# Two-bank score passes on VectorE, a re-tuned plan and a residual added on VectorE in an adaLN transformer block

## The chip, the cores and the metric

The kernel runs on one core of one Trainium2 chip. The metric is the device time of one execution in microseconds (us); less is better. Three runs of the kernel before gave 745.32, 745.73 and 746.55 us, median 745.73.

In the profile the engines are called PE (TensorE, the matmuls), PEld (its weight loads), DVE (VectorE), ACT (ScalarE), POOL (GpSimd) and SP (the engine that issues most DMAs). "L1279" is line 1279 of the kernel before.

## What is computed

A transformer block with adaptive layer norm: 2048 tokens of width 512, 32 heads of width 16, a hidden width of 1376. All inputs are bf16.

```
mod = (silu(c) @ w_mod).reshape(1, 6, 1, 512)         # sa, ca, ga, sb, cb, gb
h = layernorm(x) * (1 + ca) + sa
q, k, v = heads(h @ wqkv)
p = softmax(q k^T * 16 ** -0.5)
x = x + ga * ((p v) @ wo)
h = layernorm(x) * (1 + cb) + sb
x = x + gb * (gelu(h @ w1 + b1) @ w2 + b2)
```

## The kernel before, in words

**Streams and tiles.** The attention is cut into 32 streams, numbered `qi` 0 to 31. One stream is one block of 512 queries (four blocks `b`), one chunk of eight heads (four chunks `ch`), and the even or the odd heads of it; the four heads of a stream lie in four row groups of TensorE. The last four streams (`halved`) are cut otherwise: 256 queries, even and odd heads together. A stream has 16 key tiles of 128 keys. One tile (stream, key tile) gives four PSUM banks of scores, 128 keys x 512 queries each, one for each head. In all there are 32 x 16 = 512 tiles. The softmax is taken without its maximum: the exponential of the scores is multiplied with the values, which carry a column of ones for the sum, and the sum divides later.

**Two ways to the exponential.** Most tiles are done by ScalarE: PE writes two score banks (`issue_unit`, L991; matmuls at L923), and one ScalarE instruction takes the exponential of both (L1279, `act`). The banks of ScalarE are the pairs 0, 1 and 3, 4. The other tiles, chosen from the six key tiles in `DKT`, are done by VectorE: PE writes one score bank at a time into one of the "flex" banks 2, 5, 6 and 7 (`d_next` and `d_issue`, L946 to L982), and VectorE turns it into 16-bit integers, whose bits read as float16 are roughly the exponential (`p_pass`, L1338, instruction at L1350). When the four rows of a tile are done, three shifted copies of it are made by adding an integer (`emit_shift`, L1301; on VectorE at L1321, on GpSimd at L1327), and all four versions are multiplied with values scaled to match (`VE` and `VV`), so that the error of the rough exponential averages out. A tile on VectorE so takes four value matmuls for each row where one on ScalarE takes one. The flex banks also hold the output accumulators of the streams (`open_o`) and the banks of all other matmuls (`x_open`).

**Who decides the order.** The order of the instructions is written by a planner while the kernel is built: a small simulation (loop at L1530) with a clock for PE, ScalarE, VectorE and GpSimd and fixed costs for each operation (L54 to L78). At each step the engine that is free first picks its next work by a fixed policy: `pe` (L1154), `act`, `dve` (L1486), `pool`. VectorE takes copies of finished outputs first, then evacuations of other matmuls, then reciprocals, score passes, tasks and last shifts. GpSimd takes a shift only where VectorE has at least `POOL_MIN` us of other work in sight. What the chip then runs is this fixed order on each engine, with semaphores between them; which tile is done by ScalarE and which by VectorE is fixed by it too.

Around the attention the planner places the projections, layer norms, the up and down projections of the three earlier query blocks ("jobs" with matmuls, "tasks" without). Each has a gate, a position in the row of tiles from which it may start (`K_GATE`, `Q_GATE`, `X1_GATE`, `U_GATE`, `OUT_GATE`, `U2_GATE`, `OUT2_GATE`, `Z_GATE`). The thresholds of the policy are constants that a table may overrule for single turns; a turn (`next_turn`, L828) is half a stream of tiles, so the table `TURNS` (L38) has keys from 0 to 63:

- `D_AHEAD`: how early, before VectorE is out of work, PE may give a turn to scores for VectorE alone (L1172)
- `D_WAIT`: how much time PE must have until ScalarE needs its next banks for it to do so (L1173)
- `D_STOP`: how many tiles of a stream must be left for VectorE to begin one (L960)
- `OPEN_N`: how many value matmuls must be ready for the next stream's accumulator to be opened (L1029)
- `X_LEAD`: shifts the position against which gates are compared (L839)

**Pairs.** `p_pass` already has the code for passes over two banks: where the next waiting bank is ready, is the next higher one (`i + 1`), and holds the next row of the same tile, one instruction does both. `PAIR = False` (L85) turns it off. In the planner a pass costs 0.602 us and a pair 1.135 us.

**Fills.** Where PE has nothing to do for a while, `fill` (L1098) issues four matmuls with zero weights into an open accumulator. It needs all four rows of that stream to have started.

**The tail.** `last_tail` (L1581) does what is left after the last exponential, written out by hand, with a generator of filler matmuls (the up and down projections of the first 256 of the last 512 tokens), of which `gap(GAPS[i])` issues so many at each place. For the last two token tiles of 128 (`tt` 2 and 3) the output projection starts before the end of the attention, in the jobs "z" (L792): `outer` adds the residual `x` by a matmul with the identity and then the first three head chunks, in one bank for each token tile (`pz`). In the tail the last chunk is added (L1637, `W_z`), so that the bank holds the whole new `x`. VectorE takes the layer norm statistics straight from the bank (L1640), GpSimd the root (L291, L292), and the two tiles are normalised from the banks by ScalarE (L1648) and VectorE (L1649) side by side. After transposes and copies (L1655 to L1658) VectorE casts the two banks into `xr` (L1661), which the last adds read (L1683).

Of the kernel before, what the change touches and what calls it, by code (L numbers as in the profile page):

```python
# [21 lines left out]
P = 128  # L22
# [14 lines left out]

TURNS = {29: {'D_AHEAD': 0.3}, 30: {'D_AHEAD': 0.3}, 31: {'D_AHEAD': 0.3}, 32: {'D_AHEAD': 0.3}, 47: {'OPEN_N': 10}, 48: {'OPEN_N': 10}, 60: {'D_STOP': 5}, 61: {'D_STOP': 5}, 62: {'D_STOP': 5}, 63: {'D_STOP': 5}}  # L38
TURN = 2
# [7 lines left out]
D_FROM = 0  # L47
D_AHEAD = 0.1
D_STOP = 4
# [34 lines left out]
Q_POOL = False  # L84
PAIR = False  # L85
K_GATE = (-1.7, 0.25)
Q_GATE = -1.1
X1_GATE = (0.3, 1.3)
U_GATE = (1.7, 5.0)
OUT_GATE = (5.0, 7.9)  # L90
OPEN_N = 14
# [8 lines left out]
NARROW = False  # L100
GAPS = (10, 4, 0, 12, 2, 3, 9, 3)
NHQ = 4
# [4 lines left out]
XA_AT = 30.5  # L107
U2_GATE = (1.7, 5.0)
OUT2_GATE = (4.6, 7.2)
LOAD_AT = (2, 3)  # L110
D_END = 6
BULK_LEFT = 8
Z_GATE = 0.2

# [49 lines left out]
def adaln_block(ctx: ExitStack, tc: tile.TileContext, A_x, A_wqkv, A_wo, B_x, B_w1, B_b1, B_w2, B_b2,  # L164
# [81 lines left out]
    def bank(i):  # L246
        return PS[:, i, :]
# [82 lines left out]
    def copy(eng, dst, src):  # L330
        if eng == AC:
            nc.scalar.copy(out=dst, in_=src)
        else:
            nc.vector.tensor_copy(out=dst, in_=src)
# [332 lines left out]
    def plain(ps, lhsT, rhs, start, stop):  # L667
        nc.tensor.matmul(out=ps, lhsT=lhsT, rhs=rhs, start=start, stop=stop)  # L668
# [123 lines left out]
    for tt in range(2, 4):  # L792
        job(("z", tt), NQ - Z_GATE + 0.001 * tt, ["xl1"] + [ot_key(ch, 1) for ch in range(3)],
            [lambda ps, tt=tt, i=i: outer(bank(ps), tt)[i]() for i in range(4)], [], mode="full")
    xa, ha = hT[:, 0:2, 0:512], hT[:, :, 512:768]
# [25 lines left out]
    dcount = [0] * NQ  # L821
    st = {"ap": 0, "cur": None, "mode": None, "unit": 0, "lastpe": 0.0, "expd": 0}

# [17 lines left out]
    def halved(qi):  # L841

        return qi >= NQ - NHQ
# [310 lines left out]
    def pe(now):  # L1154
# [426 lines left out]
    def last_tail():  # L1581
# [57 lines left out]
        for t in range(2):  # L1639
            nc.vector.bn_stats(out=st2[:, 2 + t, :], in_=bank(pz[t]))  # L1640
# [8 lines left out]
        nc.vector.tensor_scalar(out=hns[0], in0=bank(pz[0]), scalar1=mv[:, 0, 0:1], scalar2=rs[:, 0:1],  # L1649
                                op0=ALU.subtract, op1=ALU.mult)  # L1650
        both = [PS[:, k, :].bitcast(BF16).rearrange("p (j n) -> p j n", n=256) for k in (kd, kr)]
# [193 lines left out]
```

## Time and profile before

| what | us |
|---|---|
| median of three runs | 745.73 |
| the profiled execution, its own time | 744.98 |
| span of its profile, first to last instruction | 743.1 |
| start of the first exponential of the attention | 13.0 |
| start of the last exponential | 716.31 |
| VectorE's score passes (L1350), first and last start | 52.8, 707.0 |

The span is what the engines show; the profiled execution's own time is 1.9 us more. A row of the page's groups reads: line, engine, operation, output and inputs with their shapes, how many; then busy time in all and the mean of one in ns; then the idle time of the engine just before these instructions and what ended most of it. A row of the timeline begins with its start and its length in us. A row of a stretch gives its length, and for each engine the busy time and the number of instructions in it, then the granted clock of TensorE as a share of full speed, the share of DMA and GB/s.

### The profile page before, as it was taken

To read this page: it belongs to the slowest core of one execution; us is meant where nothing else is said; L and a number is where in the kernel's file an instruction comes from. 1 tells how busy PE (TensorE), PEld (TensorE's weight loads), DVE (VectorE), ACT (ScalarE), POOL (GpSimd) and SP (SyncE) were. 2 spreads that over 40 slices of the span, in tenths; PEclk is the share of its full clock that TensorE was granted. 3 is DMA by queue.
4 is the path that set the end of the run, shared out by engine and by line. 5 is a ranking of instruction groups with operands and counts; after the bars stand their busy time and mean duration, and the time that the engine had idled before them with its cause. 6 is when DMAs were issued, how large, how long until landed. Compare 5 with 4: busy or idle time off the path is not lost.

```text
span 743.1 us, 22039 instructions
## 1 busy us (share of the span) xinstructions
PE 726.6 (98%) x9017; PEld 236.6 (32%) x9020; DVE 681.2 (92%) x1188; ACT 718.4 (97%) x776; POOL 421.5 (57%) x263
## 2 busy tenths in 40 slices
PE   8999999999999999999999999999999999999998
PEld 3323323232333222222222222322232222434455
DVE  8958899999999999999999999999999999989973
ACT  4999999999999999999999999999999999999993
POOL 3102756766565566676777465765667668653620
PEclk9999999999999999999999999999999999999999
DMA  8600001011120100001200200000010200000111
GB/s 279 168 10 2 25 4 24 22 56 48 45 65 11 38 10 22 7 16 24 53 17 10 44 4 15 12 18 24 18 50 5 46 10 9 19 27 22 41 27 32
DMA packets 42859, 25.57 MB, mean 34 GB/s; under 512 B 27609, under 2 KB 37906, under 8 KB 42754
## 3 DMA queue, kind: packets, MB, share of 16 engines
q1 hardware_dynamic: 41938, 23.01, 11.8%
q8 instruction: 72, 1.18, 0.6%
q10 hardware_dynamic: 816, 1.12, 0.4%
q14 instruction: 33, 0.27, 0.1%
HBM read 16.58 MB, written 2.61 MB: 26 GB/s over the span
## 4 chain that ended last, share of the span: by engine, by line
ACT 51%; PE 36%; issue 9%; DVE 3%; POOL 1%; DMA 0%; ACTq 0%; POOLq 0%; DVEq 0%
ACT pB L1279 25%; ACT pA L1279 25%; PE PS L1087 12%; PE PS L923 12%; PE PS L254 8%; PE PS L668 3%; DVE t L1350 1%; DVE t L1321 1%; POOL t L1327 1%; ACT uG L728 1%; DVE qm L341 1%; PE PS L1104 1%; DMA cc_bf<-in_c_dram 0%; DVE st L281 0%; PE PS L300 0%
## 5 line engine op out<-in xcount | busy, mean ns | idle before, releaser
L1327 POOL TENSOR_SCALAR t<-t 128x2048 int16<-128x2048 int16 x192 | 363.2, 1897 | 244.1 <-DVE t L1321 112.1
L1279 ACT ACTIVATE pA<-PS 128x1024 bf16<-128x1024 f32 x368 | 397.6, 1080 | 2.3 <-PE PS L923 1.8
L1279 ACT ACTIVATE pB<-PS 128x1024 bf16<-128x1024 f32 x368 | 398.2, 1082 | 0.4 <-PE PS L923 0.3
L1350 DVE TENSOR_SCALAR t<-PS 128x512 int16<-128x512 f32 x576 | 370.7, 680 | 26.9 <-PE PS L923 23.9
L923 PE MATMUL PS<-qm,kT 32*128 32x512 bf16 x2048 | 305.1, 383 | 7.3 <-ACT pA L1279 2.6
L1087 PE MATMUL PS<-t,VV 128*32 128x512 f16 (+1 forms) x1956 | 225.0, 359 | 1.7 <-POOL t L1327 1.6
L923 PEld LDWEIGHTS <-kT 32*128 32x128 bf16 x2048 | 86.8, 91 | 286.4 <-issue 282.3
L1321 DVE TENSOR_SCALAR t<-t 128x2048 int16<-128x2048 int16 x240 | 175.1, 755 | 0.5 <-PE PS L1087 0.2
L1087 PE MATMUL PS<-pA,VE 128*32 128x512 bf16 (+1 forms) x826 | 168.3, 361 | 0.0
L1087 PE MATMUL PS<-pB,VE 128*32 128x512 bf16 (+1 forms) x826 | 164.3, 361 | 0.0
L1087 PE MATMUL PS<-t,VE 128*32 128x512 f16 (+1 forms) x652 | 133.8, 359 | 1.4 <-DVE o_sb L1386 1.0
L1087 PEld LDWEIGHTS <-VE 128*32 128x32 bf16 x2304 | 70.1, 94 | 77.5 <-issue 72.6
L1087 PEld LDWEIGHTS <-VV 128*32 128x32 bf16 x1956 | 64.7, 95 | 58.3 <-issue 52.0
L254 PE MATMUL PS<-h2T,W 128*32 128x512 bf16 x528 | 42.7, 383 | 0.0
L254 PE MATMUL PS<-W,uG 128*32 128x512 bf16 x528 | 41.6, 394 | 0.0
L1104 PE MATMUL PS<-kT,zeros 128*32 128x512 bf16 x296 | 28.4, 383 | 0.0
L1465 POOL TENSOR_TENSOR OT<-o_sb,rb 128x512 bf16<-128x512 f32 (+1 forms) x17 | 20.0, 1177 | 14.5 <-DVE t L1321 11.8
L719 DVE TENSOR_SCALAR uG<-PS,b1c 128x512 bf16<-128x512 f32 x33 | 24.5, 742 | 1.7 <-PE PS L254 1.4
L341 DVE TENSOR_SCALAR qm<-PS,qmask 128x512 bf16<-128x512 f32 x32 | 22.6, 741 | 2.2 <-PE PS L254 2.2
L291 POOL TENSOR_SCALAR rs<-mv 128x4 f32<-128x4 f32 (+1 forms) x10 | 3.7, 371 | 34.6 <-DVE mv L286 34.1
L254 PE MATMUL PS<-hT,W_k 128*32 128x512 bf16 x256 | 21.2, 383 | 0.5 <-DVE hT L324 0.5
L254 PE MATMUL PS<-hT,W_q 128*32 128x512 bf16 x256 | 20.9, 383 | 0.0
(132 smaller groups left out, 362.9 us busy)
## 6 DMA issues: line engine op xcount, KB each, us to landing
rb<-d SPq DMA_DIRECT2D x112, 32.0 KB
W_m<-in_w_mod_dram SPq DMA_DIRECT2D x2, 1024.0 KB
out_dram<-ob SPq DMA_DIRECT2D x15, 128.0 KB
o_sb<-o SPq DMA_DIRECT2D x56, 32.0 KB
xb<-in_A_x_dram SPq DMA_DIRECT2D x3, 512.0 KB
xr<-in_A_x_dram SPq DMA_DIRECT2D x3, 512.0 KB
W<-in_B_w_dram SPq DMA_DIRECT2D x4, 344.0 KB
W<-in_B_w_dram SPq DMA_DIRECT2D x5, 256.0 KB
```

Source lines behind the costliest of these rows:

```text
L254: nc.tensor.matmul(out=ps[32 * g:32 * g + 32, :], lhsT=lhsT[:, 32 * g:32 * g + 32], rhs=rhs, start=start, stop=stop)
L341: nc.vector.tensor_scalar(out=qm[(b, ch)][:, par, :], in0=ps, scalar1=qmask[:, par:par + 1], scalar2=None, op0=ALU.mult)
L668: nc.tensor.matmul(out=ps, lhsT=lhsT, rhs=rhs, start=start, stop=stop)
L719: nc.vector.tensor_scalar(out=X["u"][:, fc, :], in0=bank(ps), scalar1=late["b1c"][:, fc:fc + 1], scalar2=None, op0=ALU.add)
L923: nc.tensor.matmul(out=dst, lhsT=kT[rows, ch, kt * P:(kt + 1) * P], rhs=rhs, start=True, stop=True)
L1087: nc.tensor.matmul(out=bank(O[qi])[32 * r:32 * r + 32, cs], lhsT=w, rhs=rhs[:, cs], start=(n == 1 and not halved(qi)), stop=last and (pr = ...
L1104: nc.tensor.matmul(out=bank(O[qi])[32 * r:32 * r + 32, :], lhsT=zeros[:, 0:32], rhs=kT[:, 0, 0:512], start=False, stop=False)
L1279: nc.scalar.activation(out=t[:, 0:n, :], in_=PS[:, b0:b0 + n, :], func=ACT.Exp, scale=math.log(2.0) / STEP)
L1321: nc.vector.tensor_scalar(out=t16[:, rs, :], in0=d["tile"][:, rs, :], scalar1=float(MJ[j]), scalar2=None, op0=ALU.add)
L1327: nc.gpsimd.tensor_scalar(out=t16[:, rs, :], in0=d["tile"][:, rs, :], scalar1=1.0, scalar2=float(MJ[j]), op0=ALU.mult, op1=ALU.add)
L1350: nc.vector.tensor_scalar(out=d["tile"][:, r:r + n, :], in0=PS[:, i:i + n, :], scalar1=T_BIAS, scalar2=0.0, op0=ALU.add, op1=ALU.max)
L1465: nc.gpsimd.tensor_tensor(out=ot[:, 0:w], in0=o[:, 0:w], in1=rb[:, 0:w], op=ALU.mult)
```

## The change

- `PAIR = True`: one VectorE pass over two neighbouring banks where both are ready.
- Constants anew: `D_AHEAD` 0.2 for 0.1, a little in the gates, `GAPS` with one filler matmul moved from the late place to the place ahead of the transposes, and another table `TURNS`: entries for turns 17 to 20, 37 to 40, 45, 46 and 55 to 59 in place of 29 to 32, 47, 48 and 60 to 63.
- The residual of the last two token tiles: the identity matmul in `outer` goes; in the tail VectorE adds bank and `xr` into `xr`, takes the statistics from there, and normalises both tiles from there; the product for ScalarE's bias, ScalarE's normalisation and the two casts go.
- `extra_fill`: where PE has been idle for over 0.3 us and nothing else was possible, four zero matmuls into the accumulator of one of the last four streams, also where not all its rows have started. The planner's clock doesn't count them.

```diff
-TURNS = {29: {'D_AHEAD': 0.3}, 30: {'D_AHEAD': 0.3}, 31: {'D_AHEAD': 0.3}, 32: {'D_AHEAD': 0.3}, 47: {'OPEN_N': 10}, 48: {'OPEN_N': 10}, 60: {'D_STOP': 5}, 61: {'D_STOP': 5}, 62: {'D_STOP': 5}, 63: {'D_STOP': 5}}
+TURNS = {17: {'D_WAIT': 0.8}, 18: {'D_WAIT': 0.8}, 19: {'D_WAIT': 0.8}, 20: {'D_WAIT': 0.8}, 45: {'D_AHEAD': 0.4}, 46: {'D_AHEAD': 0.4}, 37: {'X_LEAD': -0.1}, 38: {'X_LEAD': -0.1}, 39: {'X_LEAD': -0.1}, 40: {'X_LEAD': -0.1}, 55: {'D_WAIT': 0.7}, 56: {'D_WAIT': 0.7, 'POOL_MIN': 0.8}, 57: {'D_WAIT': 0.7}, 58: {'D_WAIT': 0.7, 'X_LEAD': 0.1}, 59: {'X_LEAD': 0.1}}
-D_AHEAD = 0.1
+D_AHEAD = 0.2
-PAIR = False
-K_GATE = (-1.7, 0.25)
-Q_GATE = -1.1
+PAIR = True
+K_GATE = (-1.7, 0.22)
+Q_GATE = -1.2
-U_GATE = (1.7, 5.0)
-OUT_GATE = (5.0, 7.9)
+U_GATE = (1.7,4.8)
+OUT_GATE = (4.6, 7.8)
-GAPS = (10, 4, 0, 12, 2, 3, 9, 3)
+GAPS = (10, 4, 0, 12, 2, 3, 8, 4)
-U2_GATE = (1.7, 5.0)
-OUT2_GATE = (4.6, 7.2)
+U2_GATE = (1.7,4.6)
+OUT2_GATE = (4.6,7.4)
-Z_GATE = 0.2
+Z_GATE = 0.6
...
     def outer(ps, tt):
-        return [lambda: plain(ps, ident, XL["xr"][:, tt, :], True, False)] + [
-            lambda ch=ch: plain(ps, ot_cols(ch, tt), W_o[:, ch, :], False, False) for ch in range(3)]
+        return [lambda ch=ch: plain(ps, ot_cols(ch, tt), W_o[:, ch, :], ch == 0, False) for ch in range(3)]
...
         if idle > 0.15 and fits(MM, "col") and fill(now):
             return True
+        if idle > 0.3 and now > st["extra"] + 0.3:
+            extra_fill(now)
         return False
+
+    def extra_fill(now):
+        for qi in sorted(O):
+            rs = [r for r in range(4) if emitted[qi][r] != total(qi)]
+            if halved(qi) and rs:
+                for r in rs:
+                    nc.tensor.matmul(out=bank(O[qi])[32 * r:32 * r + 32, :], lhsT=zeros[:, 0:32],
+                                     rhs=kT[:, 0, 0:512], start=False, stop=False)
+                st["extra"] = now
+                STATS["extra"] = STATS.get("extra", 0) + 1
+                return
...
         for t in range(2):
-            nc.vector.bn_stats(out=st2[:, 2 + t, :], in_=bank(pz[t]))
+            nc.vector.tensor_tensor(out=xr[:, 2 + t, :], in0=bank(pz[t]), in1=xr[:, 2 + t, :], op=ALU.add)
+            ln_stats(xr, st2, 2 + t)
...
-        nb = small.tile([P, 2], FP32, name="nb")
-        nc.vector.scalar_tensor_tensor(out=nb, in0=mv[:, 0:2, 0], scalar=-1.0, in1=rs[:, 0:2], op0=ALU.mult,
-                                       op1=ALU.mult)
         hns = [otp.tile([P, 512], BF16, name="OT") for _ in range(2)]
-        nc.scalar.activation(out=hns[1], in_=bank(pz[1]), func=ACT.Identity, bias=nb[:, 1:2], scale=rs[:, 1:2])
-        nc.vector.tensor_scalar(out=hns[0], in0=bank(pz[0]), scalar1=mv[:, 0, 0:1], scalar2=rs[:, 0:1],
-                                op0=ALU.subtract, op1=ALU.mult)
+        for t in range(2):
+            nc.vector.tensor_scalar(out=hns[t], in0=xr[:, 2 + t, :], scalar1=mv[:, t, 0:1], scalar2=rs[:, t:t + 1],
+                                    op0=ALU.subtract, op1=ALU.mult)
...
-        for t in range(2):
-            copy(DV, xr[:, 2 + t, :], bank(pz[t]))
```

More of the change, by code (lines that the diff above doesn't have):

```diff
@@ L793, in adaln_block @@
         job(("z", tt), NQ - Z_GATE + 0.001 * tt, ["xl1"] + [ot_key(ch, 1) for ch in range(3)],
-            [lambda ps, tt=tt, i=i: outer(bank(ps), tt)[i]() for i in range(4)], [], mode="full")
+            [lambda ps, tt=tt, i=i: outer(bank(ps), tt)[i]() for i in range(3)], [], mode="full")
     xa, ha = hT[:, 0:2, 0:512], hT[:, :, 512:768]
@@ L821, in adaln_block @@
     dcount = [0] * NQ
-    st = {"ap": 0, "cur": None, "mode": None, "unit": 0, "lastpe": 0.0, "expd": 0}
+    st = {"ap": 0, "cur": None, "mode": None, "unit": 0, "lastpe": 0.0, "expd": 0, "extra": 0.0}
     V = dict(D_AHEAD=D_AHEAD, D_STOP=D_STOP, OPEN_N=OPEN_N, D_WAIT=D_WAIT, POOL_MIN=POOL_MIN, X_LEAD=0.0)
```

## Prediction

> **What bounds the kernel now.** I read the page's first and fifth parts first, to see which engine has no slack.
>
> ```profile
> span 743.1 us, 22039 instructions
> PE 726.6 (98%) x9017; PEld 236.6 (32%) x9020; DVE 681.2 (92%) x1188; ACT 718.4 (97%) x776; POOL 421.5 (57%) x263
> ACT 51%; PE 36%; issue 9%; DVE 3%; POOL 1%; DMA 0%; ACTq 0%; POOLq 0%; DVEq 0%
> L1327 POOL TENSOR_SCALAR t<-t 128x2048 int16<-128x2048 int16 x192 | 363.2, 1897 | 244.1 <-DVE t L1321 112.1
> L1279 ACT ACTIVATE pA<-PS 128x1024 bf16<-128x1024 f32 x368 | 397.6, 1080 | 2.3 <-PE PS L923 1.8
> L1279 ACT ACTIVATE pB<-PS 128x1024 bf16<-128x1024 f32 x368 | 398.2, 1082 | 0.4 <-PE PS L923 0.3
> L1350 DVE TENSOR_SCALAR t<-PS 128x512 int16<-128x512 f32 x576 | 370.7, 680 | 26.9 <-PE PS L923 23.9
> L1321 DVE TENSOR_SCALAR t<-t 128x2048 int16<-128x2048 int16 x240 | 175.1, 755 | 0.5 <-PE PS L1087 0.2
> ```
>
> ScalarE does 368 + 368 = 736 exponentials and is idle for only 2.3 + 0.4 = 2.7 us before all of them. Each takes two score banks, a tile of one stream and key tile has four, so ScalarE does 736/2 = 368 tiles; VectorE does 576/4 = 144; together they are the 32 x 16 = 512 tiles of the kernel. PE is called 98% busy, but that share is of modelled ends and holds fill matmuls, so the dense ScalarE is what I count by. The second view is the busy time by stage, which also gives what one exponential costs in place.
>
> ```profile
> 200.00:300.00 100.00, 98.66 (x1189) 29.96 (x1187) 95.16 (x160) 99.99 (x109) 62.95 (x40) 1.00 0.12 29
> 300.00:400.00 100.00, 98.03 (x1190) 28.43 (x1190) 94.94 (x151) 99.87 (x104) 69.16 (x39) 1.00 0.08 21
> 500.00:600.00 100.00, 99.44 (x1197) 28.45 (x1195) 97.49 (x166) 99.99 (x109) 64.94 (x36) 1.00 0.11 28
> 716.31 1.18 ACT L1279 ACTIVATE pB<-PS 128x1024 bf16<-128x1024 f32 x1
> 717.51 1.28 ACT L1623 ACT_TABLE_LOAD   x1
> ```
>
> The columns are PE, weight loads, DVE, ACT, POOL. ScalarE is full; 109 exponentials fill 100 us, 0.917 us each (the 1.08 of the page overlaps the next one). The last one ends at 716.31 + 1.18 = 717.49, and what follows is the tail to 743.1. So the time is a head, a dense row of exponentials, and a tail. **The time moves by 2 x 0.917 = 1.83 us for every tile that changes hands between ScalarE and VectorE**, and hardly by anything else in the middle. VectorE, which limits how many tiles leave ScalarE, is idle for 4.8, 5.1 and 2.5 us of those three stretches, about 4.1 us in 100.
>
> **The change part by part.** *Two-bank passes.* What VectorE pays for a tile: four passes, and 240 of the 432 shifts (POOL does the other 192), so 240/144 = 1.67; back to back either takes about 0.6 us, as the fence below shows for the passes (1.29 - 0.69 = 0.60). That is 4 x 0.60 + 1.67 x 0.60 = 3.4 us. A pass over 1024 columns is not in the trace; the nearest rows are one operation from PSUM at two widths, and runs of single passes.
>
> ```profile
> L1683 DVE TENSOR_TENSOR ob<-PS,xr 128x256 bf16<-128x256 f32 x2 | 0.8, 425 | 1.3 <-PE PS L668 1.3
> L1683 DVE TENSOR_TENSOR ob<-PS,xr 128x512 bf16<-128x512 f32 x1 | 0.7, 691 | 1.8 <-PE PS L668 1.8
> 309.75 1.29 DVE L1350 TENSOR_SCALAR t<-PS 128x512 int16<-128x512 f32 x2 [0.21 <-PE PS L923]
> 315.97 1.29 DVE L1350 TENSOR_SCALAR t<-PS 128x512 int16<-128x512 f32 x2 [0.49 <-PE PS L923]
> 317.75 0.69 DVE L1350 TENSOR_SCALAR t<-PS 128x512 int16<-128x512 f32 x1 [0.49 <-PE PS L923]
> L1350 DVE TENSOR_SCALAR t<-PS x576: 623/680/693, 52.8 to 707.0; 128x512 int16<-128x512 f32 x192
>   PE PS L923: 23.9, 64
> ```
>
> 256 more columns cost 691 - 425 = 266 ns, so 1024 columns cost 691 + 532 = 1223 ns against 1.29 us for two passes: a pair saves 0.06 us. How many pairs there are is in the order the planner writes, not in the trace: walking the passes of the kernel before, I find 36 places where the next pass is already ready, on the next row of the same tile and in the next higher bank. 36 x 0.06 = 2.2 us, or 2.2/3.4 = 0.6 tile. Against that stands a wait. Single passes give the first bank back while the second is being read, so PE can write new scores into it; a pair gives both back at its end. The last row of the fence (idle time of VectorE before L1350, and how often) says what such a wait costs where it happens today: 23.9/64 = 0.37 us. Behind the waiting pass stand, in VectorE's fixed order, shifts and the copies that empty PE's other banks, and PE's value matmuls wait for those. If every pair brought one wait, 36 x (0.37 - 0.06) = 11 us or 3.3 tiles would be lost; if none did, 0.6 is gained. I take a wait behind every second pair: 18 x 0.37 - 2.2 = 4.5 us, 1.3 tiles, in whole tiles **one tile back to ScalarE, +1.83 us**, ends -1.1 and +6.0 us.
>
> [...]
>
> *Plan constants and the table for single turns.* They move gates and thresholds of the planner, add no kind of instruction, and no row prices them one by one. What they can move is the number of tiles, 1.83 us each. The bound is VectorE's idle time: 4.1 in 100 us over the stage from 52.8 us (its first pass) to 707 is 27 us, 27/3.4 = 8 tiles if all were used, and as many lost if it doubled. I take none for the sum and half of that, 3.5 tiles either way, for the range. The two places I can read point both ways: waiting longer before PE gives a turn to VectorE's scores (D_WAIT 0.7 and 0.8 in eight turns) starves VectorE, issuing earlier (D_AHEAD 0.2 for 0.1) feeds it.
>
> *The last residual.* These are the rows of the tail's path now, then the rows that price what replaces them.
>
> ```profile
> 721.66 0.69 DVE L1640 BATCH_NORM_STATS2 st<-PS 128x6 f32<-128x512 f32 x1
> 722.23 0.59 PE L668 MATMUL PS<-W_z,OT 128*128 128x512 bf16 x2
> 722.86 0.70 DVE L1640 BATCH_NORM_STATS2 st<-PS 128x6 f32<-128x512 f32 x1 [0.51 <-PE PS L668]
> 724.16 0.71 POOL L292 TENSOR_TENSOR rs<-rs,mhalf 128x2 f32<-128x2 f32 x1
> 724.99 0.81 DVE L1649 TENSOR_SCALAR OT<-PS,mv,rs 128x512 bf16<-128x512 f32 x1
> 725.85 0.50 PEld L1655 LDWEIGHTS <-OT 128*128 128x128 bf16 x8 [0.27 <-DVE OT L1649]
> 726.97 1.28 DVE L334 CAST xr<-PS 128x512 bf16<-128x512 f32 x2
> 737.47 0.69 DVE L1683 TENSOR_TENSOR ob<-PS,xr 128x512 bf16<-128x512 f32 x1 [1.83 <-PE PS L668]
> L694 DVE TENSOR_TENSOR xr<-PS,xr 128x512 bf16<-128x512 f32 x12 | 8.2, 682 | 0.4 <-PE PS L254 0.3
> L281 DVE BATCH_NORM_STATS2 st<-xr 128x6 f32<-128x512 bf16 x12 | 8.2, 681 | 0.1
> 714.21 0.73 DVE L783 TENSOR_SCALAR OT<-hT,mv,rs 128x512 bf16<-128x512 bf16 x2 [0.92 <-POOL rs L292]
> 716.36 0.39 PE L668 MATMUL PS<-xr,ident 128*128 128x512 bf16 x1
> ```
>
> Now the last projection lands at 722.23 + 0.59 = 722.82 and its statistics end at 723.56. After: add 721.66 to 722.34, statistics to 723.02, second add from 722.95 to 723.63, statistics to 724.31: 0.75 us later. From the root (724.87) to the end of the last normalised tile is 0.93 us now; two normalisations from SBUF take 0.73, with 0.04 to start, and the small product for ScalarE's bias goes: 0.16 us back. Net 0.59. One filler matmul more is put ahead of the transposes (0.2 us, what the second of two adds to 0.39 in the row of W_z), which can hide part: **+0.5 us**, ends 0.38 and 0.75. The two identity matmuls (0.2 us each in place) and the two casts count nothing: PE waits there for the exponential that ends at 717.49, and the casts lie beside the up projection, and their output is first read by the add at 737.47. Without that cover the matmuls would be worth 0.4 us. If the later transposes expose the copies behind them, these are late next.
>
> *Extra fills.* They can run only in the last four streams, when PE has been idle for over 0.3 us. There is one place that they fit.
>
> ```profile
> 650.19 0.40 PE L1051 MATMUL PS<-zeros 128*32 128x512 bf16 x4 [0.18 <-DVE t L1350]
> 651.38 0.39 PE L923 MATMUL PS<-qm,kT 32*128 32x512 bf16 x2 [0.79 <-DVE o_sb L1386]
> 648.00:656.00 8.00, 6.38 (x74) 2.37 (x74) 7.08 (x12) 7.96 (x5) 3.50 (x3) 0.84 0.03 6
> 656.00:664.00 8.00, 8.00 (x116) 2.55 (x120) 6.56 (x12) 7.55 (x9) 5.08 (x3) 0.94 0.10 28
> 656.11 1.03 ACT L1279 ACTIVATE pA<-PS 128x1024 bf16<-128x1024 f32 x1
> 660.56 1.02 ACT L1279 ACTIVATE pA<-PS 128x1024 bf16<-128x1024 f32 x1
> ```
>
> While ScalarE runs the third GELU, PE has gaps, the granted clock (the third number from the end) falls to 0.84 and 0.94 in these stretches, from 1.00 in those above, and the four exponentials from 656.11 to 660.56 take 4.45 us where 4 x 0.917 = 3.67 would do: 0.8 us lost. The new plan puts that GELU at another place among other work, so I take 0, ends -0.8 and 0. [...]
>
> **Sum.** +1.83 + 0 + 0.5 + 0 = +2.3 us. The profiled execution took 744.98 us (span 743.1), so it would take 747.3; the median of the runs shown, 745.73, is 0.75 above it: **748.1 us**, with 738 exponentials.
>
> **The rivals.** *Faster: VectorE gains tiles.* If pairs bring no waits and the constants use part of its idle time, two tiles go over (6.8 us of 27), -3.7 us, + 0.5 for the tail, -0.4 for half of the dip: 742.1 us. It decides at one tile gained. For it: 27 us are idle and the 0.06 is real. Against: 36 places are few, and nothing else of the change makes VectorE's work smaller.
>
> *No difference: it does not pair.* Where the planner finds hardly any neighbouring ready banks and the constants cancel, 736 exponentials stay and only the tail is left: 746.2 us. For it: 540 of 576 passes found no such neighbour.
>
> *Much slower: pairs starve VectorE.* With every pair followed by a 0.37 us wait and the constants as badly off by one tile, four tiles go back: +7.3 + 0.5 = 753.5 us. For it: the only long waits of VectorE are already for PE's scores. Against: it has shifts to do in between, and the planner puts them there.
>
> **How the numbers follow.** A measurement of this kernel can tell about 0.2% (1.5 us) from no change. Forecast, one or two tiles lost, 0.43; much slower 0.15; no difference 0.15; faster 0.27. So slower 0.58, same 0.15, faster 0.27. The range: low is 3.5 - 1 = 2.5 tiles gained (-4.6), tail 0.4, dip -0.8: 740.7; high is 4.5 tiles lost (+8.2) and tail 0.75: 754.7. The signs are split, so the forecast's own range is 747.9 to 750.1: one tile with a tail of 0.38, two with 0.75.
>
> **What would show it.** The count of exponentials decides: 738 or more of L1279 is the forecast, 734 or fewer the faster rival, and the last one should end near 719.3 us. In L1350's rows, 128x1024 forms should number about 36 at 1.22 us; the wait before L1350 should be above 26.9 us if pairs starve it. From the end of the last exponential to the end of the span should be 26.1 us, 0.5 more than 25.6 now. The clock in the third GELU's stretch shows the fills. I am wrong if the exponentials are fewer, if ScalarE shows idle time beyond 2.7 us, or if the tail does not grow.

## The result and the profile after

| what | before | after |
|---|---|---|
| median of 21 runs | 745.86 us | 748.40 us |
| profiled execution, span | 743.1 us | 746.6 us |
| last exponential ends | 717.49 us | 716.35 us |
| from there to the end of the span | 25.6 us | 30.2 us |
| exponentials on ScalarE | 736 | 734 |

The ratio is 1.0032, with a 95% interval of 1.0019 to 1.0045: slower by 0.3%. The forecast of 748.1 us came out almost to the number, and the profile shows that it did so for a wrong reason: the forecast's count was 738 exponentials or more, and "I am wrong if the exponentials are fewer" was one of its signs. The page of the kernel after, its span, engines and costliest groups:

```profile
span 746.6 us, 22132 instructions
PE 726.7 (97%) x9075; PEld 236.6 (32%) x9078; DVE 681.1 (91%) x1153; ACT 717.0 (96%) x773; POOL 424.0 (57%) x264
L1291 ACT ACTIVATE pA<-PS 128x1024 bf16<-128x1024 f32 x367 | 393.1, 1071 | 2.2 <-PE PS L922 2.0
L1291 ACT ACTIVATE pB<-PS 128x1024 bf16<-128x1024 f32 x367 | 393.5, 1072 | 0.2
L1362 DVE TENSOR_SCALAR t<-PS 128x512 int16<-128x512 f32 (+1 forms) x539 | 370.6, 721 | 26.6 <-PE PS L922 23.2
L1103 PE MATMUL PS<-kT,zeros 128*32 128x512 bf16 x332 | 31.7, 382 | 0.0
```

The count that was to decide stands in the second and third group: 367 + 367 = 734 exponentials, two fewer than before. VectorE did not lose a tile, it gained one (367 tiles on ScalarE, 145 on VectorE), and its idle time before the passes is 26.6 us, not above the 26.9 of before. The last row is `fill`, 332/4 = 83 calls; the line of `extra_fill` has no row at all, so that edit issued nothing. The two forms of the passes, from the groups with shapes kept apart:

```profile
L1362 DVE TENSOR_SCALAR t<-PS 128x512 int16<-128x512 f32 x498 | 323.1, 680 | 23.8 <-PE PS L922 21.0
L1362 DVE TENSOR_SCALAR t<-PS 128x1024 int16<-128x1024 f32 x41 | 49.8, 1215 | 2.8 <-PE PS L922 2.2 <-issue 0.2
```

There are 41 pairs of 1215 ns. Two singles in a row take 680 + 600 = 1280 ns, so each pair saves about 0.065 us. Ahead of all 41 pairs VectorE is idle for only 2.8 us.

So the dense row is shorter, as the faster rival had it, and the kernel is slower. The time comes back in the tail. Here are its three stages, first before, then after: from the last exponential's end (cut at 716.36 for after, 0.01 us past it) to the first filler matmul (up projection of the first half, L668 `hT,W`), from there to PE's transposes (L1655 before, L1665 after), and the rest. The columns are PE, weight loads, DVE, ACT, POOL, then the granted clock.

```profile
717.49:718.55 1.06, 1.06 (x12) 0.43 (x12) 0.50 (x1) 1.04 (x2) 0.00 (x0) 1.00 0.38 75
718.55:725.90 7.35, 7.27 (x55) 5.32 (x56) 5.35 (x16) 5.99 (x14) 0.93 (x2) 1.00 0.01 3
725.90:743.10 17.20, 13.75 (x101) 9.36 (x101) 6.38 (x14) 5.46 (x12) 0.00 (x0) 0.97 0.11 33
```

```profile
716.36:720.18 3.82, 1.60 (x14) 0.54 (x14) 2.61 (x9) 1.49 (x2) 0.00 (x0) 1.00 0.64 73
720.18:729.40 9.22, 9.17 (x58) 6.31 (x60) 4.47 (x10) 4.97 (x11) 0.94 (x2) 0.81 0.00 1
729.40:746.60 17.20, 13.46 (x100) 9.10 (x98) 5.37 (x13) 5.46 (x12) 0.00 (x0) 0.96 0.11 34
```

The stages grew by 3.82 - 1.06 = 2.76, 9.22 - 7.35 = 1.87 and 0 us; the exponentials ended 1.13 earlier; 2.76 + 1.87 - 1.13 = 3.5, which is 746.6 - 743.1. In the first stage PE was busy for only 1.60 of 3.82 us. In the second the clock was granted at 0.81: 9.22 x 0.19 = 1.75 us lost, nearly all of the 1.87. The timeline of after names what PE waited for:

```profile
704.37 0.69 DVE L732 TENSOR_TENSOR ob<-PS,xr 128x512 bf16<-128x512 f32 x1 [0.19 <-PE PS L254]
705.95 0.61 PE L254 MATMUL PS<-W_o,OT 128*32 128x512 bf16 x8
711.41 0.68 DVE L767 TENSOR_TENSOR hT<-PS,hT 128x512 bf16<-128x512 f32 x1
715.20 1.14 ACT L1291 ACTIVATE pB<-PS 128x1024 bf16<-128x1024 f32 x1
715.42 3.45 SPq L509 DMA_TRANSPOSE hT<-OT  x2
716.81 1.25 PE L668 MATMUL PS<-W_o,OT 128*128 128x512 bf16 x5
720.18 3.38 PE L668 MATMUL PS<-hT,W 128*128 128x256 bf16 x20 [2.12 <-DMA hT<-OT]
```

and the same places before:

```profile
696.06 0.68 DVE L732 TENSOR_TENSOR ob<-PS,xr 128x512 bf16<-128x512 f32 x1
702.28 0.61 PE L254 MATMUL PS<-W_o,OT 128*32 128x512 bf16 x8
710.07 0.69 DVE L768 TENSOR_TENSOR hT<-PS,hT 128x512 bf16<-128x512 f32 x1
714.65 2.56 SPq L509 DMA_TRANSPOSE hT<-OT  x2
718.55 2.53 PE L668 MATMUL PS<-hT,W 128*128 128x256 bf16 x20
```

The first filler cannot run before `hT` of the first half of the last block (`tt` 0 and 1) has been transposed by two DMAs. That chain runs beside the exponentials: projection (L254 `W_o,OT`), residual add (L767), norm, transposes (L509), landing. Before, the transposes were issued 717.49 - 714.65 = 2.84 us ahead of the last exponential's end; after, 716.36 - 715.42 = 0.94 ahead. Counted from the start of the span, the issue is only 0.77 us later (715.42 for 714.65); the other 1.13 us of the lost lead is the earlier end of the exponentials itself, which the chain did not follow. On the chain the projection starts 3.7 us later, and its last matmul 0.9 us later (710.5 for 709.6). Ahead of it the output matmuls of the block before end later too: their last add (L732) comes at 704.37 in place of 696.06, and the planner keeps one such job open at a time (`X_MAX`). That this add held the projection up, and the projection the transposes, is argued from the plan and was not isolated; a_out2 below speaks against the projection alone.

The landing itself takes longer too. These are the two issues, before and then after, with shortest, median and longest in ns:

```profile
L509 SPq DMA_TRANSPOSE hT<-OT x2: 1195/1230/1264, 714.6 to 716.0; - x2
```

```profile
L509 SPq DMA_TRANSPOSE hT<-OT x2: 1260/1673/2086, 715.4 to 716.8; - x2
```

From the first issue to the first filler were 718.55 - 714.65 = 3.90 us, and are 720.18 - 715.42 = 4.76. (Before, PE had no wait there; where the filler does wait for a landing without the disturbance told next, the time is 3.81 us, so before had some 0.1 us to spare.) The transfers of after from 716.45 to 717.50 us hold one packet that is not data:

```profile
q1 hardware_dynamic: 500, 0.12, 146.6%
q8 instruction: 1, 0.02, 7.9%
```

Queue q8 brings instructions, 16 KB at a time and 73 times in the span. They are PE's: 9075 + 9078 records of PE and PEld make about 250 for each packet (the median between two packets is 256, before and after), and more PE instructions move the packets: 120 more put the one 1.07 us behind the issue 1.06 us ahead of it (a_shift below), 152 more the one of before from 10.6 to 1.13 us behind it (b_hit). This one starts 1.07 us after the first transpose was issued. Before, the nearest one came 1.62 us ahead of the issue, and no q8 packet lies between issue and landing. Last, the clock of after, one us at a time from 721 us, with its fall:

```profile
721.00:722.00 1.00, 1.00 (x9) 0.79 (x7) 0.06 (x1) 0.85 (x3) 0.00 (x0) 0.67 0.03 8
722.00:723.00 1.00, 1.00 (x7) 0.69 (x6) 0.00 (x0) 0.62 (x2) 0.00 (x0) 0.50 0.00 0
724.00:725.00 1.00, 1.00 (x6) 0.64 (x5) 0.55 (x1) 0.07 (x1) 0.00 (x0) 0.63 0.00 0
```

It is down for about 3.4 us, after the 2.12 us in which PE waited for the landing.

### The profile page after: what moved, and what is told of

It is laid out like the page before. It is cut to its first block, busy times and chain, and to the rows that moved or that the text cites. A ratio compares the mean times of both kernels' runs of the same rounds, so it can differ in the third digit from the quotient of the medians.

```text
span 746.6 us, 22132 instructions
## 1 busy us (share of the span) xinstructions
PE 726.7 (97%) x9075; PEld 236.6 (32%) x9078; DVE 681.1 (91%) x1153; ACT 717.0 (96%) x773; POOL 424.0 (57%) x264
## 4 chain that ended last, share of the span: by engine, by line
ACT 55%; PE 32%; issue 9%; DVE 2%; DMA 1%; POOL 0%; POOLq 0%; ACTq 0%; DVEq 0%
ACT pB L1291 27%; ACT pA L1291 26%; PE PS L922 11%; PE PS L1086 11%; PE PS L254 7%; PE PS L668 3%; ACT uG L728 1%; DVE t L1362 1%; DVE qm L341 0%; DMA hT<-OT 0%; PE PS L1103 0%; ACT L1291 0%; DMA cc_bf<-in_c_dram 0%; DVE t L1333 0%; DVE st L281 0%
## 5 line engine op out<-in xcount | busy, mean ns | idle before, releaser
L1291 ACT ACTIVATE pA<-PS 128x1024 bf16<-128x1024 f32 x367 | 393.1, 1071 | 2.2 <-PE PS L922 2.0
L1362 DVE TENSOR_SCALAR t<-PS 128x512 int16<-128x512 f32 (+1 forms) x539 | 370.6, 721 | 26.6 <-PE PS L922 23.2
L1291 ACT ACTIVATE pB<-PS 128x1024 bf16<-128x1024 f32 x367 | 393.5, 1072 | 0.2
L1086 PE MATMUL PS<-pA,VE 128*32 128x512 bf16 (+1 forms) x822 | 164.5, 362 | 0.3 <-ACT pB L1291 0.3
L1086 PE MATMUL PS<-t,VE 128*32 128x512 f16 (+1 forms) x660 | 131.5, 358 | 0.0
L254 PE MATMUL PS<-h2T,W 128*32 128x512 bf16 x528 | 43.0, 384 | 0.0
L254 PE MATMUL PS<-W,uG 128*32 128x512 bf16 x528 | 42.8, 383 | 0.0
L1103 PE MATMUL PS<-kT,zeros 128*32 128x512 bf16 x332 | 31.7, 382 | 0.0
L719 DVE TENSOR_SCALAR uG<-PS,b1c 128x512 bf16<-128x512 f32 x33 | 24.5, 742 | 1.6 <-PE PS L254 1.5
L254 PE MATMUL PS<-hT,W_k 128*32 128x512 bf16 x256 | 20.7, 384 | 0.5 <-DVE hT L324 0.5
L254 PE MATMUL PS<-hT,W_q 128*32 128x512 bf16 x256 | 21.0, 383 | 0.0
```

The costliest lines, as they stand in the source:

```text
L254: nc.tensor.matmul(out=ps[32 * g:32 * g + 32, :], lhsT=lhsT[:, 32 * g:32 * g + 32], rhs=rhs, start=start, stop=stop)
L719: nc.vector.tensor_scalar(out=X["u"][:, fc, :], in0=bank(ps), scalar1=late["b1c"][:, fc:fc + 1], scalar2=None, op0=ALU.add)
L1086: nc.tensor.matmul(out=bank(O[qi])[32 * r:32 * r + 32, cs], lhsT=w, rhs=rhs[:, cs], start=(n == 1 and not halved(qi)), stop=last and (pr = ...
L1103: nc.tensor.matmul(out=bank(O[qi])[32 * r:32 * r + 32, :], lhsT=zeros[:, 0:32], rhs=kT[:, 0, 0:512], start=False, stop=False)
L1291: nc.scalar.activation(out=t[:, 0:n, :], in_=PS[:, b0:b0 + n, :], func=ACT.Exp, scale=math.log(2.0) / STEP)
L1362: nc.vector.tensor_scalar(out=d["tile"][:, r:r + n, :], in0=PS[:, i:i + n, :], scalar1=T_BIAS, scalar2=0.0, op0=ALU.add, op1=ALU.max)
```

## The experiments

Two theories stood at the start. The first: the tail grew because the first half's transposes land late, by the new plan. Its rival: the rewritten tail (residual on VectorE, another `GAPS`) is what costs. Every kernel was timed against the kernel before on its own chip; "tail" is from the last exponential's end to the end of the span, "landing" from the first of the two L509 issues to the first filler, "fetch" the start of the nearest q8 packet to that issue (minus: ahead of it).

| kernel | ratio (95%) | exponentials | tail | landing | fetch |
|---|---|---|---|---|---|
| before | 1 | 736 | 25.6 | 3.90 | -1.62 |
| after | 1.0032 (1.0019 to 1.0045) | 734 | 30.2 | 4.76 | +1.07 |
| b_tail | 1.0001 (0.9981 to 1.0022) | 736 | 26.1 | 3.81 | -1.39 |
| a_oldtail | 1.0020 (0.9999 to 1.0041) | 734 | 28.9 | 4.57 | +1.05 |
| b_pair | 1.0034 (1.0012 to 1.0055) | 738 | 26.8 | 3.84 | -4.18 |
| a_nopair | 1.0065 (1.0044 to 1.0086) | 740 | 27.1 | 3.81 | -4.65 |
| a_warm | 1.0026 (1.0010 to 1.0043) | 734 | 28.9 | 4.84 | +0.91 |
| a_shift | 1.0002 (0.9985 to 1.0020) | 734 | 27.9 | 3.81 | -1.06 |
| b_hit | 1.0009 (0.9992 to 1.0027) | 736 | 26.7 | 5.09 | +1.13 |
| a_petr | 1.0019 (1.0001 to 1.0036) | 734 | 28.3 | no DMA | |
| a_out2 | 1.0051 (1.0032 to 1.0069) | 734 | 30.1 | 5.31 | +3.25 |
| ao_out2 | 1.0051 (1.0032 to 1.0071) | 734 | 28.5 | 5.39 | +3.27 |
| a_gate | 0.9995 (0.9981 to 1.0009) | 734 | 26.4 | 5.05 | -2.05 |
| a_gate_s | 0.9978 (0.9964 to 0.9992) | 734 | 26.3 | 5.20 | +1.26 |

The mean granted clock is known for each run too, and the same kernel takes longer where it is lower: the kernel after has 747.5 us (median of 7 runs) at 1.000 and 749.7 (5 runs) at 0.998. Where a median mixes such runs, the runs at 1.000 are compared below as well.

### b_tail: the kernel before with the new residual alone

```diff
-GAPS = (10, 4, 0, 12, 2, 3, 9, 3)
+GAPS = (10, 4, 0, 12, 2, 3, 8, 4)
...
-            nc.vector.bn_stats(out=st2[:, 2 + t, :], in_=bank(pz[t]))
+            nc.vector.tensor_tensor(out=xr[:, 2 + t, :], in0=bank(pz[t]), in1=xr[:, 2 + t, :], op=ALU.add)
+            ln_stats(xr, st2, 2 + t)
```

and the other tail lines of the change's diff.

> The kernel before with only the residual moved: no identity matmul, add, statistics and both normalisations on VectorE, and the filler moved in GAPS. 736 exponentials as before. Theory 1 (the changed kernel's tail is long because the transposes of the first half of the last block land late after the last exponential, and PE's clock halves in that wait; the residual itself costs little): +0.2 to +0.6 us against before, no wait of more than 0.5 us for hT<-OT. Theory 2 (the added pass on VectorE makes the tail long): +3 us or more, tail near 30 us.

Measured 745.70 against 745.74 us. Its timeline at the start of the tail:

```profile
716.58 1.18 ACT L1278 ACTIVATE pB<-PS 128x1024 bf16<-128x1024 f32 x1
718.72 2.54 PE L668 MATMUL PS<-hT,W 128*128 128x256 bf16 x20 [0.18 <-DMA hT<-OT]
```

The row ends at 717.76 and the tail of 26.1 is 0.5 longer than before, the predicted term. In the medians nothing of it is to be seen (a ratio that can tell some 0.2% can't resolve 0.07%); the runs at full clock, 745.5 (4 runs) against 745.2 (11), have 0.3.

### a_oldtail: the kernel after with the old residual

```diff
-        return [lambda ch=ch: plain(ps, ot_cols(ch, tt), W_o[:, ch, :], ch == 0, False) for ch in range(3)]
+        return [lambda: plain(ps, ident, XL["xr"][:, tt, :], True, False)] + [
+            lambda ch=ch: plain(ps, ot_cols(ch, tt), W_o[:, ch, :], False, False) for ch in range(3)]
```

and the old `GAPS`, statistics, normalisations and casts.

> The changed kernel with the residual of before restored (identity matmul, statistics from the bank, ScalarE's normalisation, GAPS of before). 734 exponentials. Theory 1 (late transposes and a halved clock): the wait for hT<-OT stays, tail 29 to 30 us, +1.5 to +3 us against before. Theory 2 (the residual on VectorE): the tail goes back to about 25.6 us, 1 us faster than before.

Measured 747.24 us. Its first filler:

```profile
720.18 2.36 PE L668 MATMUL PS<-hT,W 128*128 128x256 bf16 x20 [1.75 <-DMA hT<-OT]
```

With the old tail's code the tail is still 28.9 us, 3.4 above before, and the first filler still comes 3.9 us after the last exponential (716.28). The rival falls. What the tail's own edits are worth on this plan is not resolved: from the first filler to the end are 25.0 us here and 24.7 with the new code in a_warm below, both at full clock, while the medians at full clock are 747.1 us here (8 runs) and 747.5 for after (7 runs, not timed beside these). The clock did not fall in this profile; PE's wait for the landing was 1.75 us there, and 2.12 in the profile of after.

### b_pair and a_nopair: the pairs without the constants, and the reverse

```diff
-PAIR = False
+PAIR = True
```

on the kernel before, and on the kernel after

```diff
-PAIR = True
+PAIR = False
```

> The kernel before with only the passes over two banks turned on; its plan then writes 738 exponentials (143 tiles on VectorE, 52 pairs). If the row of exponentials sets the time: +1.8 us plus what the end of the new plan does to the tail (-0.5 to +3). If pairs starve VectorE, its idle time before the passes rises from 26.9 us by about 0.37 us a pair, to 40 us or more; if they don't, it stays within 24 to 30 us.

> The changed kernel with single passes only; its plan then writes 740 exponentials (142 tiles on VectorE). If the row of exponentials sets the time: last exponential 5.5 us later than in the changed kernel, and with a tail of 26 to 30 us +3.7 to +8 us against before. If pairing costs time, it would be no slower than the changed kernel (+2.5 us).

Measured 748.20 and 750.48 us. b_pair, groups with shapes kept apart and then its page:

```profile
L1350 DVE TENSOR_SCALAR t<-PS 128x1024 int16<-128x1024 f32 x52 | 63.2, 1216 | 2.8 <-PE PS L923 1.9
```

```profile
L1279 ACT ACTIVATE pA<-PS 128x1024 bf16<-128x1024 f32 x369 | 400.1, 1084 | 2.3 <-PE PS L923 2.0
L1350 DVE TENSOR_SCALAR t<-PS 128x512 int16<-128x512 f32 (+1 forms) x520 | 364.2, 733 | 26.0 <-PE PS L923 22.7
```

and a_nopair:

```profile
L1291 ACT ACTIVATE pA<-PS 128x1024 bf16<-128x1024 f32 x370 | 397.5, 1074 | 2.2 <-PE PS L922 1.8
L1362 DVE TENSOR_SCALAR t<-PS 128x512 int16<-128x512 f32 x568 | 366.5, 680 | 29.1 <-PE PS L922 26.3
```

Pairs alone make 52 pairs and still cost one tile (2 x 369 = 738 exponentials), not because VectorE starves on the chip (26.0 us idle, less than before) but because the order that the planner then writes gives it a tile less; why it does is not shown. The new constants alone cost two tiles (740) and raise the wait to 29.1 us. Both together gain one, as the 734 of after show. So neither edit has a price of its own: the constants fit the pass form they were chosen with. The row from the first exponential's start to the last one's end rises with the count: 703.3, 704.5, 705.8 and 708.8 us for 734, 736, 738 and 740, that is by 1.2 and 1.3 us for a tile and then by 3.0, on average 5.5/3 = 1.83 us for a tile.

### a_warm: is it the clock?

```diff
         nc.vector.reciprocal(out=rt, in_=den)
+        warm(9, kd)
         gap(GAPS[0])
```

Nine zero matmuls ahead of the first filler, so that PE does not wait idle for the landing.

> The changed kernel with nine matmuls of zeros on PE (1.9 us) between its last output projection and the fillers that wait for hT<-OT. The wait stays, and PE is busy in it. Theory 1a (half of the tail's extra time is TensorE's clock, halved after PE stood still for 2.1 us): the granted clock stays at 1.00 after the wait, the stage from the first filler to the transposes goes from 9.2 to about 7.7 us, -1.0 to -1.7 us against the changed kernel in executions that have the dip. Theory 1b (only the wait counts): no change, within 0.3 us.

Measured 749.10 us. The two first stages of its tail:

```profile
716.40:720.56 4.16, 3.54 (x22) 1.43 (x23) 2.64 (x9) 1.49 (x3) 0.20 (x1) 1.00 0.61 69
720.56:727.97 7.41, 7.36 (x56) 5.42 (x58) 4.18 (x10) 4.86 (x11) 0.94 (x2) 1.00 0.00 1
```

PE is busy and the clock stays at 1.00. From the first filler to the transposes are 7.41 us, where after had 9.22 and 7.7 was expected; from the first filler to the end are 24.7 us where the profile of after has 26.4. In that execution the dip was worth 1.65 us. But the median stays (1.0026 against 1.0032): at full clock a_warm has 747.50 us (4 runs) and after 747.52 (7). The dip in the tail therefore belongs to some executions, and most of what the change loses is lost without it.

### a_shift and b_hit: is it the instruction fetch?

The same fills, cut in halves, only add PE instructions, and so move the times at which PE's instructions are fetched. In a_shift (kernel after) the first 15 fills:

```diff
-                for r in rs:
-                    nc.tensor.matmul(out=bank(O[qi])[32 * r:32 * r + 32, :], lhsT=zeros[:, 0:32],
-                                     rhs=kT[:, 0, 0:512], start=False, stop=False)
+                for cs in (slice(0, 256), slice(256, 512)) if STATS.get("fills", 0) < 15 else (slice(0, 512),):
+                    for r in rs:
+                        nc.tensor.matmul(out=bank(O[qi])[32 * r:32 * r + 32, cs], lhsT=zeros[:, 0:32],
+                                         rhs=kT[:, 0, cs], start=False, stop=False)
```

b_hit is the same with 19 fills in the kernel before, to bring a fetch in where there was none.

> The changed kernel with each of its first 15 fills cut into two halves of 256 columns: 120 PE instructions more, no more matmul work, so that PE's fetch of 16 KB of instructions, seen 1.07 us after the first transpose is issued, comes about 3 us earlier and misses it. Theory 1c (that fetch delays the transposes): the two DMA issues take 2.6 us again in place of 3.45, hT<-OT lands 0.8 to 1 us earlier after its issue, -0.8 us or, where the shorter wait also spares the clock, to -2.5 us. Theory 1d (they land late only because they are issued late): no change in the 3.45 us.

> The kernel before with its first 19 fills cut into halves: 152 PE instructions more, so that the fetch that comes 10.6 us after the first transpose is issued moves to 1 to 2 us after it. Theory 1c (the fetch delays the transposes): the issues take 3.2 us or more in place of 2.56, hT<-OT lands 0.6 to 1 us later, PE waits 0.8 us more, +0.6 to +1.5 us against before. Theory 1d: no change.

Measured 747.08 and 747.19 us, on one chip with a_warm. Timeline of a_shift, then of b_hit (the clock of a_shift's profiled execution was down for 10 us near its start, which delays everything behind, so only the tail is read):

```profile
719.75 1.15 ACT L1292 ACTIVATE pB<-PS 128x1024 bf16<-128x1024 f32 x1
720.22 2.56 SPq L509 DMA_TRANSPOSE hT<-OT  x2
724.03 2.14 PE L668 MATMUL PS<-hT,W 128*128 128x256 bf16 x18 [1.41 <-DMA hT<-OT]
```

```profile
715.01 3.80 SPq L509 DMA_TRANSPOSE hT<-OT  x2
716.67 1.18 ACT L1280 ACTIVATE pB<-PS 128x1024 bf16<-128x1024 f32 x1
720.10 1.16 PE L668 MATMUL PS<-hT,W 128*128 128x256 bf16 x9 [1.03 <-DMA hT<-OT]
```

With the fetch 1.06 us ahead of the issue, two issues take 2.56 us and the landing 3.81; with a fetch 1.13 us behind it, 3.80 and 5.09. The fetch works in both directions, by 0.9 us taken from after and 1.2 added to before. At full clock a_shift has 746.66 us (8 runs), 0.84 below a_warm on the same chip; this is rough, since the eight lie in two groups, 746.0 to 746.3 and 747.1 to 747.3. For b_hit the slower landing is clear, but its ratio of 1.0009 is not clear of 1. In a_shift the landing is without a fetch and the filler still waits 1.41 us for it: what is left is the late issue.

### a_petr: the transposes without the DMA

```diff
-            task(("t2", b, tt), XA_AT, [("n2", b, tt)], "SP", 0.0,
-                 lambda t=tt: transpose_dma(ha[:, :, t * P:(t + 1) * P], hn[t]), out=(SP_T, 0.0))
...
+        job(("t2", b), XA_AT, [("n2", b, tt) for tt in range(2)],
+            [lambda ps, i=i: turn4(ps, i) for i in range(4)],
+            [((DV,), lambda eng, ps: copy(eng, ha, PS[:, ps, :].bitcast(BF16).rearrange("p (j n) -> p j n", n=256)))],
+            cost=0.23, mode="full")
```

`turn4` issues two of eight PE transposes into one bank, which VectorE copies out.

> The changed kernel with the first half's normalised tiles of the last block transposed by PE (eight matmuls into one bank, one copy by VectorE) in place of the two DMA transposes. 734 exponentials as in the changed kernel. Theory 1 (the tail is long because those transposes land 3.8 us after the last exponential): the first filler starts within 1.5 us of the last exponential, the clock stays at 1.00, tail 26 to 27.5 us, -2.5 to -4 us against the changed kernel, so 0 to -1.5 us against before. Theory 2 (the residual on VectorE makes the tail long): -0.5 us at most.

Measured 747.58 us; it missed. Its timeline:

```profile
717.61 0.61 PE L793 MATMUL PS<-ident,OT 128*128 128x128 bf16 x8
718.26 0.69 DVE L334 COPY hT<-PS 128x1024 bf16<-128x1024 bf16 x1 [1.94 <-PE PS L793]
718.92 0.72 DVE L1643 STREAM_TRANSPOSE rb<-PS 128x512 f32<-128x512 f32 x1
719.01 2.34 PE L668 MATMUL PS<-hT,W 128*128 128x256 bf16 x20
```

The filler comes 2.30 us after the last exponential, where 1.5 was expected, and the tail is 28.3 us for 26 to 27.5: PE got to the transposes only at 717.61, and in VectorE's fixed order the copy stands ahead of what empties the last output (L1643), which waits behind it. It takes the landing away and puts a wait of VectorE in its place.

### a_out2 and ao_out2: issue earlier by the old gate

```diff
-OUT2_GATE = (4.6,7.4)
+OUT2_GATE = (4.6,7.2)
```

on the kernel after; ao_out2 has the old residual besides.

> The changed kernel with one number of before put back: OUT2_GATE (4.6, 7.2) in place of (4.6, 7.4), so that the last output matmuls of the third block free PE's single slot for other matmuls earlier and the first half's projections (lines W_o,OT before the last exponential) start earlier. 734 exponentials. Theory 1 (the tail is long because the first half's chain, from those projections to the transposes, ends late): the projections start near 703 in place of 705.95 us, the transposes are issued about 1.2 us earlier, the first filler comes 1.2 to 2 us earlier after the last exponential (2 to 2.6 in place of 3.8 us), -1 to -2.5 us against the changed kernel, so within 1.5 us of before. Theory 2 (the residual on VectorE): no gain.

> The same with the residual of before as well (identity matmul, statistics from the bank, ScalarE's normalisation, GAPS of before). 734 exponentials. Theory 1: as the kernel with the gate alone, and at most 0.5 us less for the residual: 0 to -1.5 us against before. Theory 2: 1 us or more faster than the kernel with the gate alone.

Measured 749.88 and 749.11 us, both missed. These are the first fillers of a_out2 and of ao_out2, each with a stretch behind it:

```profile
721.67 0.50 PE L668 MATMUL PS<-hT,W 128*128 128x256 bf16 x3 [2.71 <-DMA hT<-OT]
723.00:724.00 1.00, 1.00 (x7) 0.67 (x6) 0.00 (x0) 0.62 (x2) 0.00 (x0) 0.50 0.03 8
```

```profile
723.05 2.36 PE L668 MATMUL PS<-hT,W 128*128 128x256 bf16 x20 [2.35 <-DMA hT<-OT]
723.05:726.00 2.95, 2.95 (x25) 2.46 (x26) 0.77 (x3) 2.16 (x5) 0.00 (x0) 1.00 0.01 3
```

In a_out2 the transposes were issued 1.72 us ahead of the last exponential's end (718.08), 0.8 earlier than in after, but a fetch fell into the landing (+3.25 us) and it took 5.3 us, so the filler was 3.6 us late all the same. The projection started at 701.44 us, 4.5 us earlier than in after, and ended earlier as well (last matmul at 709.4 for 710.5), so it is not the projection alone that sets the issue. The clock behind the wait fell to 0.50 in a_out2 and stayed at 1.00 in ao_out2. Besides, the first exponential started at 14.8 us in the profile of a_out2 where after has 13.1: there PE waits up to 1.9 us for the load of `W_m`, which after does not. The profiles of b_pair, ao_out2 and a_gate have this wait too, and a_gate_s, with the constants of a_gate, does not, so it does not come with those constants; why the load is late stays open.

### a_gate and a_gate_s: issue early enough

```diff
-OUT2_GATE = (4.6,7.4)
+OUT2_GATE = (4.4,7.3)
...
-D_END = 6
+D_END = 4
```

`D_END` is the number of tiles that must be left at the end of the attention for VectorE to begin one. a_gate_s has the first 16 fills cut in halves besides, as in a_shift.

> The changed kernel with OUT2_GATE (4.4, 7.3) and D_END 4: 734 exponentials as in the changed kernel, but the plan puts the first half's projections about 5 us earlier. Theory 1 (the tail begins when the first half's transposes have landed, not with the last exponential): the transposes are issued 3 us or more before the last exponential ends, the first filler comes within 1.2 us of it where PE's fetch of instructions misses them and within 2.2 us where it hits, tail 25.3 to 27 us; -1 to -1.6 us against before without a hit, -0.5 to +0.3 with one. Theory 2 (the residual on VectorE makes the tail long): tail near 30 us, as in the changed kernel.

> The same with the first 16 fills cut into halves: 128 PE instructions more, half of one fetch of 256. Theory 1c (a fetch of PE's instructions within about 0.9 to 3.3 us of the first transpose's issue delays them by 0.7 to 1.5 us): the time from that issue to the first filler is 3.8 to 3.9 us in the one of the two kernels whose fetch misses and 4.6 us or more in one whose fetch hits, unless the last exponential ends later than the transposes land in both. Theory 1d (the fetch has no part): the same in both.

Measured 745.47 and 744.86 us, against 746.04 on their chip. **a_gate_s is faster than both kernels: 0.9978 (0.9964 to 0.9992)** of before, where after has 1.0032; a_gate's interval still holds 1, and its gain is less than the 1 to 1.6 us expected. The timeline of a_gate_s:

```profile
713.11 3.92 SPq L509 DMA_TRANSPOSE hT<-OT  x2
715.34 1.14 ACT L1292 ACTIVATE pB<-PS 128x1024 bf16<-128x1024 f32 x1
718.31 2.36 PE L668 MATMUL PS<-hT,W 128*128 128x256 bf16 x20
```

The issue is 3.4 us ahead of the last exponential's end, and the filler waits for no DMA any more, although a fetch fell in (3.92 us for the two issues). The tail is 26.3 us, close to the 26.1 of before with the new residual, and the row, which ends 1.0 us earlier than before (716.48), is a gain again. The halved fills moved a fetch into the landing here, and in a_gate none falls there before the data are in place: the last data packet of the transposes ends 4.74 us after the first issue here and 3.44 us after it in a_gate (whose next fetch starts 4.60 us after it), but the fillers start 1.83 and 1.69 us after the last exponential. Where the issue is this early, the fetch costs nothing that can be seen. (The filler of a_gate was expected within 1.2 us.) At full clock the two agree, 744.74 (5 runs) and 744.81 (8), both 0.9 below before (745.66, 9 runs), so the fills add nothing there; a_gate's higher median goes with a clock of 0.997 or less in 5 of its 12 runs; a_gate_s had none so low. Why is open.

## Why the prediction was right in size and wrong in its steps

- **One tile back to ScalarE, +1.83: failed.** A tile was gained, -1.13 us at the end of the row (the price of 1.83 a tile holds only on average over 734 to 740). The step that failed is "a wait behind every second pair". The saving of 0.06 us was right (0.065 measured), the pairs were nearly as many as counted (41 for 36; 52 with the old constants), but where the step had 18 x 0.37 = 6.7 us of new waits, the passes as a whole wait 26.6 us for 26.9, and 26.0 in b_pair, where the pairs alone were turned on.
- **The constants, 0 by themselves: failed as a separate term.** Alone they cost two tiles; pairs alone cost one; together they gain one. They can't be priced apart.
- **A tail that starts with the last exponential: the missing step, and the largest.** The prediction carried the tail of before over and added the residual to it. The wait for the first half's transposes was a row of before as well, hidden because the landing ended just as PE had done its last matmuls behind the row. 2.76 us came from there: 1.9 by the later issue (0.94 for 2.84 us ahead) and 0.86 by the slower landing (4.76 for 3.90). Of the 1.9, 1.13 is the very time by which the row got shorter: the tail began when the landing ended, so the tile gained bought nothing, and the issue itself was 0.77 later. a_oldtail shows that it is not the tail's code, a_shift takes the 0.9 off, and in a_gate_s, where two constants move other work of the plan too, the wait is gone.
- **The residual, +0.5: right on the kernel before.** b_tail's tail has 26.1 for 25.6. On the kernel after it is not resolved: a_warm's stages after the first filler have 24.7 for 24.5 before, but a_oldtail's, with the old code, 25.0.
- **Extra fills, 0: right, and more simply than thought.** None was issued. The dip beside the third GELU (in before a clock of 0.50 for 3.4 us from 653.5 us) stands in the three profiles with the plan of before (before, b_tail, b_hit) and in none of the others; another came in the tail, where the prediction did not look. Whether such fills would have ended the dip was therefore not tried.
- **The rivals.** "Faster" had its condition met, one tile gained, and the other sign; it lacked the same step. "Pairs starve VectorE" and "it does not pair" are refuted by the rows of L1362.

At full clock after has 747.5 us and before 745.1 to 745.7 on four chips, +1.9 to +2.5 us. The row gives -1.1, the landing +2.8, the residual, by b_tail, +0.3 to 0.5: +2.0 to +2.2. In the profiled spans the dip comes on top, with 1.75 of the 3.5 us, and leaves 0.1 for the residual. That the sum of the prediction was +2.3 is a coincidence of a wrong loss and an overlooked one. Open stay how much of the median the late issue and the fetch each bear (the one profile has 1.9 and 0.86), and how often the tail's dip occurs.

## What to carry over

A shorter row on the busiest engine is a gain only if the first work behind the row is ready that much earlier: look up what that work waits for, follow it back beyond the end of the row, and note how many us of slack it has (here about 0.1 us was left before the change). Constants that a planner was tuned with belong to the instruction costs they were tuned on; change and judge them together. A transfer on which the start of a stage hangs should be issued with a few us to spare, since instruction fetches that no line of the program names can fall into it (here 4.57 to 5.39 us from issue to first filler where one did and the filler waited, for 3.81 to 3.90; issued 3.4 us ahead of the last exponential's end, in a_gate_s, the transfers were not waited for).

## What the runs showed of the hardware

A DMA transpose under way took longer here where a fetch of PE's instructions came into it. Over the kernels here, issue to first filler is 3.81 to 3.90 us where the nearest fetch starts ahead of the issue, and 4.57 to 5.39 where it starts 0.9 to 3.3 us after it; where it starts within 1.3 us, the second issue on SP takes 1.9 to 2.6 us in place of 1.2. (In a_gate and a_gate_s the filler does not wait for the landing, so their 5.05 and 5.20 belong to neither group.) The transfers say the same for all 13 kernels with these DMAs: the last data packet ends 3.42 to 3.47 us after the first issue without such a fetch (a_gate among them) and 4.09 to 4.74 with one (a_gate_s among them). Packets of another instruction queue, q14, start 0.9 to 1.0 us after the issue in a_shift and a_gate as well, without such a delay, so it is not they. The fetches are the packets of q8: 73 in the span of after, 1.20 MB in all, 16.4 KB each.

TensorE's clock fell to 0.50 after PE had stood still for 2.12 us (after) and 2.71 us (a_out2), and did not after 1.75 us (a_oldtail), nor after 2.35 us in ao_out2, whose clock stayed at 1.00. So the length of the pause alone does not decide; what else does was not shown. Executions of one kernel differ in it too: of the 21 of after, 7 have a mean clock of 1.000 and 5 of 0.998, which is what one dip makes (3.4 us at half clock in 746.6).
